# Row counts and queue order of the k, v, q and weight transfers in a fused attention and feed-forward kernel

## The chip, the cores and the metric

The kernel runs on one core of one Trainium2 chip. The metric is the device time of that core in microseconds, as the median of three runs. A profile is one further execution, recorded instruction by instruction and DMA packet by packet; its own span is 926.5 us.

## The reference

The program is a linear attention followed by a feed-forward block with a gated activation, in float32:

```python
kv  = einsum('bhsd,bhse->bhde', k, v)             # q, k, v: 8 x 8 x 576 x 64
out = einsum('bhsd,bhde->bhse', q, kv)
x   = out / sqrt(mean(out*out, -1) + 1e-6) * g_norm   # then (b,h,s,d) -> (b*s, h*d): 4608 x 512
h   = x @ w_in                                    # 512 x 2048
g   = h * erf(softplus(h))
y   = g @ w_out                                   # 2048 x 512
```

The weights reach the chip as 64-bit floats and are turned into float32 on the chip, which is why w_in and w_out are first read as pairs of 32-bit words (`w_raw`).

## The kernel before

**Tiles.** The batch of eight sequences gives nine token blocks T of 512 tokens (T = 0 to 7 hold the first 512 tokens of a sequence each, T = 8 holds the eight rests of 64). The 512 model columns are four chunks of 128, each a pair of heads; a "pair" is one T and one of its four head pairs, numbered i = 4 T + p. The 2048 hidden columns are 16 blocks f of 128.

**Two ways to multiply.** T = 0, the first two hidden blocks of T = 1 and the output of T = 1's first twelve use plain float32 matmuls and weights kept on the chip (`w_in_sb`, `w_out_sb`). Everything after that works on operands split into three forms, and a product of 512 x 128 x 512 is twelve matmuls: eight into `n_ps` and four into `m_ps` (`product`, L634). The three forms of each weight block are one tile of 128 rows of 6144 bytes (768 KB). They are made once during T = 1 (`w_upper` on ScalarE, `w_lower` on VectorE), stored to DRAM by `w_lower` (L672, or L668 for those kept in `w_in_sb`'s place), and read back for every token block by `load_parts` (L773).

**Periods.** From T = 2 on the work goes in 28 periods of four hidden blocks: m counts them, each T has four. In a period TensorE makes four hidden products (`hidden`, weights from `w_in_parts`) and then four result products (`result`, one for each 128 tokens j; each reads all four `w_out_parts` tiles of the batch of hidden blocks made a period before). Between these come pieces of the attention of the pair (T + 1, p) with p the period's number in its block: `visit` multiplies q by the kv matrix and forms the kv matrix of the next pair, `mean` and `norm` normalise, `turn` transposes the next pair's q on VectorE (L318). Which piece goes where is a list of places. In the first period of a block the four results of the block before are stored (`store`, L705).

**Buffers.** w_in_parts has four buffers: the tile of hidden block f is replaced once its product is done. w_out_parts has seven; a batch's four tiles come free together, at the end of the period's last product, since each of the four results reads all four tiles. k, v and q have two buffers for each pair in turn.

**Order of the transfers.** All of these are issued by SyncE's queue (SP), in the order in which the program is written; an instruction of SP that waits holds all that stand behind it. The strings in `FETCH` say after which of the eight products of a period a weight tile is asked for: "in" at places 1, 2, 4 and 6, "out" at 3, 5 and twice at 7, and four w_out tiles ahead of the first period. `load_pair` asks for k and v of the pair two ahead, and `load_q` (eight small transfers of 32 x 8 x 32 or 32 x 10 x 32 elements, 128 bytes a piece) for its q, at the attention's third group of pieces (places 3). In T = 0 and T = 1 they are asked for in the middle of a hidden block's work.

**Shapes of k and v.** For T > 0 the 576 rows of k are dealt out as five chunks (`chunks`): 115 rows hold five consecutive tokens each, and the one token left over is a row of its own, the second transfer of `load_pair` (L146). `kv_products` multiplies the rows in two halves, 0 to 63 and the rest. For T = 0 there are six chunks of 96 rows and no rest.

Of the kernel before, what the change touches and what calls it, by code (L numbers as in the profile page):

```python
# [49 lines left out]

BATCH = 4
LAG = 5


FIRST = 2
# [6 lines left out]
def kernel(  # L62
# [48 lines left out]
    exp_ln_table()  # L111


    q_sb, k_sb, v_sb = {}, {}, {}


    q_last = early.tile([P, 2, 2, D], FP32, name="q_last", bufs=1)
# [2 lines left out]

        return 6 if T == 0 else 5

    def load_pair(i, turned=True):
        T, p = divmod(i, NP)
        if T >= B:
            return
        pool = early if i in (2, 3) else kvp
        side = nc.scalar if i < 3 else nc.sync
        if T == 0:
            t = pool.tile([P, G if pool is early else S], FP32, name="q_sb", tag="q")  # L130
            t = q_sb[T, p] = t[:, 0:G].rearrange("p (j h d) -> p j h d", j=J, h=2)
            nc.sync.dma_start(
                out=t, in_=q[T, 2 * p : 2 * p + 2, 0:G, :].rearrange("h (p j) d -> p j h d", j=J)
            )
        for name, got, src in (("k", k_sb, k), ("v", v_sb, v)):
            C = chunks(T)
            rows, rest = divmod(S, C)
            assert rest < 2
            t = got[T, p] = pool.tile([rows + rest, 2, C, D], FP32, name=f"{name}_sb", tag=name)
            heads = src[T, 2 * p : 2 * p + 2]  # L140
            side.dma_start(
                out=t[:rows].rearrange("r h c d -> r h (c d)"),
                in_=heads[:, : S - rest].rearrange("h (r c) d -> r h (c d)", c=C),
            )
            if rest:
                side.dma_start(  # L146
                    out=t[rows:, :, 0], in_=heads[:, S - rest :].rearrange("h r d -> r h d")
                )
        if T > 0 and turned:
            load_q(i)  # L150

    def load_q(i):


        T, p = divmod(i, NP)
        t = q_sb[T, p] = kvp.tile([P, S], FP32, name="q_sb", tag="q")
        for n in range(P // SQ):
            h, w = divmod(n, D // SQ)
            to = t[n * SQ : n * SQ + SQ].rearrange("a (j b) -> a j b", b=SQ)
            for head, js in ((1 - h, slice(0, G // 2 // SQ)), (h, slice(G // 2 // SQ, S // SQ))):  # L160
                src = q[T, 2 * p + head, :, w * SQ : w * SQ + SQ]
                nc.sync.dma_start(
                    out=to[:, js], in_=src.rearrange("(j a) b -> a j b", a=SQ)[:, js]
                )

    def load_last(p):
        nc.sync.dma_start(
# [152 lines left out]
    def kv_products(T, p, at, crossed):  # L320


        ks, vs = (x.pop((T, p)) for x in (k_sb, v_sb))
        C = chunks(T)
        for c in range(C):
            for r in range(2):
                rows = (slice(0, D), slice(D, S // C + (c < S % C)))[r]
                for i in range(2):
                    yield partial(
                        nc.tensor.matmul,  # L330
                        at[rows_of[i], 1 - (r ^ i) if crossed else r, kv_cols],
                        lhsT=ks[rows, i, c],
                        rhs=vs[rows, i, c],
                        start=(c == 0),
                        stop=(c == C - 1),
                    )
# [29 lines left out]
    def attention(T, p, pools=None, in_parts=False):  # L366
# [31 lines left out]
        def products():  # L398

            kv_ps = st["kv"] = bank("kv_ps")  # L400
            ks, vs, qs = (x.pop((T, p)) for x in (k_sb, v_sb, q_sb))
            C = chunks(T)
            for c in range(C):
                rows = slice(0, S // C + (c < S % C))
                for i in range(2):
                    s = rows_of[i]
                    nc.tensor.matmul(
                        kv_ps[s, s],
                        lhsT=ks[rows, i, c],
                        rhs=vs[rows, i, c],  # L410
                        start=(c == 0),
                        stop=(c == C - 1),
                    )
            if p % 2 == 0:
                nc.tensor.transpose(kv_ps[:, q_tail], q_last[:, p // 2], ident)
            st["qT"] = square_tile("qT")
            for s in rows_of:
                nc.vector.tensor_copy(out=bd[s, s], in_=kv_ps[s, s])
            if p % 2 == 0:
                tails[T] = attp.tile([P, G], FP32, name="qT_last", tag="sq_lo")[:, 0:P]  # L420
                nc.vector.tensor_copy(out=tails[T], in_=kv_ps[:, q_tail])
            st["tail"] = tails[T][:, p % 2 * R : p % 2 * R + R]
            qt_ps = bank("qt_ps")
            for j in range(J):
                nc.tensor.transpose(qt_ps[:, j * P : j * P + P], qs[:, j], ident)
            nc.scalar.copy(st["qT"], qt_ps)
# [123 lines left out]
            split_lower()  # L550

        def loads():
            load_pair(T * NP + p + 2)

        if T == 0:
            return products, apply, halve, mean, norm
# [4 lines left out]
        first_ = (partial(prepare, T, p),) if (T, p) == (1, 0) else ()  # L561
        then_ = partial(turn, *then)
        if apart:
            pieces = (first_, (visit, halve, keep_tail), (loads, then_))
            return (*(partial(chain, *group) for group in pieces), mean, norm, *after)
        pieces = (first_, (visit, loads), (halve, keep_tail) if halves else (keep_tail,))
        return (*(partial(chain, *group) for group in pieces), mean, partial(chain, norm, then_), *after)
# [176 lines left out]
    for i in range(NP + 3):  # L744
        for piece, p in ((0, i), (1, i - 1), (4, i - 3), (3, i - 2)):
            if 0 <= p < NP:
                first[p][piece]()
        if i == 1:
            for _ in range(RAW - 2):
                w_next("load")  # L750
            load_pair(NP, turned=False)
            load_pair(NP + 1, turned=False)
        for what in w_rounds.get(i, ()):
            w_next(what)


    w_late.append(True)
    load_q(NP)
    first_batch, batches = FIRST * NB, NG * NB
    w_seq = {  # L760
        which: [(which, f) for _ in range(NG - FIRST) for f in range(FC)] for which in ("in", "out")
# [3 lines left out]
    def load_parts(which, n):  # L765


        pool = w_out_p if which == "out" and len(w_seq["out"]) > BATCH else w_in_p
        for _ in range(n):
            if w_seq[which]:  # L770
                key = w_seq[which].pop(0)
                t = pool.tile([P, 3, G], FP32, name=f"w_{which}_parts", tag="w")
                nc.sync.dma_start(out=t, in_=w_kept[key])  # L773
                w_now.setdefault(key, []).append(t)
# [47 lines left out]
    for n in range(FIRST * FC + 1):  # L822
# [58 lines left out]
        if T < FIRST:  # L881
            if n == whole:
                old_h = acc.tile([P, BATCH, G], FP32, name="h", tag="e")
            h = hs[n] = old_h[:, n - whole] if n >= whole else unit("h_sb")
            s = ss[n] = unit("s_sb")
            if n in plain:
                nc.scalar.copy(h, plain.pop(n))
            else:
                nc.scalar.activation(h, n_ps, AF.Copy, scale=SHIFT - 1.0)
                add(h, m_ps)  # L890
            if T == FIRST - 1:
                if f == 1:
                    x_both = wide.tile([P, KC, G], FP32R, name="x_both", tag="b")
                    for i in range(0, KC, 2):
                        both_only(x_high[:, i : i + 2], x_low[:, i : i + 2], x_both[:, i : i + 2])
                    x_forms[T] = x_high, x_low, x_both
                gates(done)
                for key in list(w_new):
                    w_lower(*key)
                for key in to_cut[f]:  # L900
                    w_upper(*key)
            nc.scalar.activation(s, h, AF.Softplus)
            if n == 0:
                w_next("split")
            if n == 1:
                load_q(NP + 1)
            for piece in steps[f][1]:
                piece()
            if f % BATCH == BATCH - 1:
                for i in range(n - BATCH + 1, n + 1):  # L910
                    nc.scalar.activation(ss[i], ss[i], AF.Erf)  # L911
                softplus_table()
            if T == FIRST - 1:
                load_parts("in", {FC - 3: 2, FC - 2: 1, FC - 1: 1}.get(f, 0))
# [9 lines left out]
        if T < FIRST:  # L924
            for piece in steps[f][2]:
                piece()
    for n in range(whole, FIRST * FC):
        gates(n)

# [3 lines left out]
    ctx.enter_context(tc.tile_pool(name="shift_r", bufs=1, side="right")).tile([P, 496], FP32, name="shift_r")  # L933
    late_r = ctx.enter_context(tc.tile_pool(name="late_r", bufs=1, side="right"))
    gate_r = ctx.enter_context(tc.tile_pool(name="gate_r", bufs=1, side="right"))
    w_out_p = ctx.enter_context(tc.tile_pool(name="w_out_p", bufs=7, side="right"))

    def part(h, half):
        return h[:, :, half * 2 * P : half * 2 * P + 2 * P]
# [30 lines left out]
                store(T, j, es[j], cols)  # L970


    FETCH = ("", "in", "in", "out", "in", "out", "in", "out out")
    load_parts("out", BATCH)
    g_next = []
    for m in range(first_batch, batches + 1):
        T, b = divmod(m, NB)
# [9 lines left out]
        def piece():  # L987
            if todo:
                todo.pop(0)()
# [13 lines left out]
                todo.pop(0)()  # L1003

        def fetch(place):
            for which in FETCH[place].split():
                load_parts(which, 1)


# [101 lines left out]
```

## Time and profile before

| | |
|---|---|
| median of three runs | 926.72 us (926.64 to 927.29) |
| profiled span | 926.5 us |
| HBM read, written | 224.40 MB, 34.60 MB |
| DMA packets, of these under 512 bytes | 143210, 78936 |
| SP's queue waiting for TensorE before a weight tile (L773, m_ps) | 190.9 us in 79 waits |
| SP's queue waiting for v before a q transfer (L162) | 38.6 us in 26 waits |

The page of a profile gives the busy time of each engine (PE is TensorE, PEld its weight loads, DVE VectorE, ACT ScalarE, SPq SyncE's queue). A line of a timeline begins with the start and the length in us; what stands in brackets at its end is the time for which the engine was idle before it, and what ended this. A line of the list of waits gives who waited for whom, the us in total, how often, and the longest.

### The profile page before, as it was taken

The numbers are of one execution on the slowest core, as the hardware profiler recorded it, in microseconds if no ns is written. First come the engines' busy times: TensorE is split into PE (matmuls) and PEld (weight loads), VectorE is DVE, ScalarE is ACT, GpSimd is POOL, SyncE is SP. The second block draws the span as 40 slices with busy tenths as digits, with TensorE's granted clock in tenths as the row PEclk, the third lists the DMA queues.
The fourth block names the chain that finished last, engine by engine and source line by source line (L and its number), as shares of the span: only waits on it lengthen the run. The fifth ranks groups of instructions, "written<-read, shape, count | busy, mean of one in ns | idle before, by whom it ended". The sixth has DMA issues, their size and how long they took to land.

```text
span 926.5 us, 13591 instructions
## 1 busy us (share of the span) xinstructions
PE 898.8 (97%) x4990; PEld 668.6 (72%) x4990; DVE 751.0 (81%) x1088; ACT 589.9 (64%) x783; POOL 2.4 (0%) x10
## 2 busy tenths in 40 slices
PE   6999999988999999999999999999999999999998
PEld 4444445655587888778878888788878888888886
DVE  2799958888588888888888888888888888886777
ACT  3868766767675666656665666666666766665552
POOL 1000000000000000000000000000000000000000
PEclk9999999999999999999999999999999999999999
DMA  9767506698688888988898788887889788778871
GB/s 250 237 190 265 167 1 249 246 378 313 239 287 312 311 312 310 347 308 308 308 337 309 296 310 310 301 306 284 292 313 404 272 286 322 291 288 314 325 271 51
DMA packets 143210, 259.91 MB, mean 281 GB/s; under 512 B 78936, under 2 KB 101800, under 8 KB 143144
## 3 DMA queue, kind: packets, MB, share of 16 engines
q1 hardware_dynamic: 141432, 256.74, 75.7%
q10 hardware_dynamic: 1648, 2.29, 0.9%
q8 instruction: 40, 0.66, 0.3%
q14 instruction: 26, 0.21, 0.1%
q0 software_dynamic: 64, 0.00, 0.0%
HBM read 224.40 MB, written 34.60 MB: 280 GB/s over the span
## 4 chain that ended last, share of the span: by engine, by line
PE 76%; DMA 11%; DVE 6%; ACT 5%; issue 1%; SPq 1%; DVEq 0%; ACTq 0%
PE n_ps L634 41%; PE m_ps L634 20%; PE o_ps L690 6%; PE h_ps L874 4%; DMA w_out_parts<-w_out 4%; DMA w_in_parts<-w_in 2%; DMA w_in<-w_new 2%; DMA v_sb<-in_v_dram 1%; PE at_ps L449 1%; PE at_ps L435 1%; DMA w_raw<-in_moe_w_out_dram 1%; ACT s_sb L911 1%; DMA q_sb<-in_q_dram 1%; DVE h L612 1%; PE at_ps L496 1%
## 5 line engine op out<-in xcount | busy, mean ns | idle before, releaser
L634 PE MATMUL n_ps<-w_out_parts,g_forms 128*128 128x512 f32 x928 | 231.2, 391 | 1.7 <-DMA w_out_parts<-w_out 1.7
L634 PE MATMUL n_ps<-x_forms,w_in_parts 128*128 128x512 f32 x896 | 225.1, 393 | 3.2 <-DMA w_in_parts<-w_in 2.1
L634 PEld LDWEIGHTS n_ps<-w_out_parts,g_forms 128*128 128x128 f32 x928 | 172.4, 188 | 38.4 <-DMA w_out_parts<-w_out 3.3
L634 PEld LDWEIGHTS n_ps<-x_forms,w_in_parts 128*128 128x128 f32 x896 | 166.1, 188 | 41.1 <-ACT h L1024 3.2
L1039 ACT ACTIVATE s<-h 128x512 f32<-128x512 f32 x112 | 71.0, 634 | 180.9 <-DVE h L612 180.9
L612 DVE TENSOR_TENSOR h<-m_ps,h 128x512 f32<-128x512 f32 x116 | 79.9, 689 | 61.5 <-ACT h L1024 39.9
L634 PE MATMUL m_ps<-w_out_parts,g_forms 128*128 128x512 f32 (+1 forms) x468 | 124.3, 388 | 0.0
L634 PE MATMUL m_ps<-x_forms,w_in_parts 128*128 128x512 f32 x448 | 119.8, 389 | 0.0
L690 PE MATMUL o_ps<-w_out_sb,h_sb 128*128 128x512 f32 x224 | 101.5, 596 | 0.2 <-DVE h_sb L820 0.2
L634 PEld LDWEIGHTS m_ps<-w_out_parts,g_forms 128*128 128x128 f32 x468 | 87.5, 188 | 18.4
L634 PEld LDWEIGHTS m_ps<-x_forms,w_in_parts 128*128 128x128 f32 x448 | 84.1, 188 | 17.6
L612 DVE TENSOR_TENSOR e<-m_ps,e 128x512 f32<-128x512 f32 (+1 forms) x117 | 80.3, 687 | 14.1 <-PE m_ps L634 2.9
L1024 ACT ACTIVATE h<-n_ps 128x512 f32<-128x512 f32 x112 | 65.6, 585 | 16.6 <-PE n_ps L634 16.6
L690 PEld LDWEIGHTS o_ps<-w_out_sb,h_sb 128*128 128x128 f32 x224 | 41.3, 189 | 45.3 <-issue 42.8
L578 DVE SCALAR_TENSOR_TENSOR g_forms<-g_forms 128x1024 fp32r<-128x1024 f32 x58 | 71.1, 1225 | 2.0
L575 DVE TENSOR_TENSOR g_forms<-h,g_forms 128x1024 fp32r<-128x1024 f32 x58 | 70.6, 1217 | 1.2 <-ACT g_forms L572 1.1
L572 ACT ACTIVATE g_forms<-h 128x1024 fp32r<-128x1024 f32 x58 | 58.7, 1051 | 14.8 <-PE m_ps L634 10.9
L1071 DVE TENSOR_TENSOR h<-h,s 128x1024 f32<-128x1024 f32 x56 | 65.9, 1218 | 0.0
L874 PE MATMUL h_ps<-xT,w_in_sb 128*128 128x512 f32 x144 | 64.6, 594 | 0.0
L607 DVE SCALAR_TENSOR_TENSOR e<-n_ps,e 128x512 f32<-128x512 f32 x88 | 60.1, 683 | 1.5 <-PE n_ps L634 1.5
L109 ACT ACT_TABLE_LOAD x44 | 56.5, 1283 | 0.8
L874 PEld LDWEIGHTS h_ps<-xT,w_in_sb 128*128 128x128 f32 x144 | 27.1, 190 | 33.4 <-issue 31.6
(119 smaller groups left out, 990.7 us busy)
## 6 DMA issues: line engine op xcount, KB each, us to landing
w_out_parts<-w_out SPq DMA_DIRECT2D x116, 768.0 KB
w_in_parts<-w_in SPq DMA_DIRECT2D x112, 768.0 KB
w_in<-w_new SPq DMA_DIRECT2D x16, 768.0 KB
w_raw<-in_moe_w_in_dram SPq DMA_DIRECT2D x16, 512.0 KB
w_raw<-in_moe_w_out_dram SPq DMA_DIRECT2D x8, 1024.0 KB
out_dram<-e SPq DMA_DIRECT2D x32, 256.0 KB
k_sb<-in_k_dram SPq DMA_DIRECT2D x28, 287.5 KB
v_sb<-in_v_dram SPq DMA_DIRECT2D x28, 287.5 KB
```

The source lines that it names most:

```text
L109: nc.scalar.preload_act_table_set("softplus")
L572: nc.scalar.activation(high, x, AF.Copy, scale=1.0 + 2.0**-13)
L575: nc.vector.tensor_tensor(out=low, in0=x, in1=high.bitcast(FP32), op=ALU.subtract)
L578: nc.vector.scalar_tensor_tensor(out=both, in0=low.bitcast(FP32), scalar=SHIFT, in1=high.bitcast(FP32), op0=ALU.mult, op1=ALU.add,)
L607: nc.vector.scalar_tensor_tensor(out=out_, in0=ps, scalar=scale, in1=out_, op0=ALU.mult, op1=ALU.add)
L612: nc.vector.tensor_tensor(out=out_, in0=ps, in1=out_, op=ALU.add)
L634: nc.tensor.matmul(ps[:, cols], lhsT=weights(form, k), rhs=moving(form, k)[:, cols], start=(form == forms[0] and k == 0), stop=(form == fo ...
L690: nc.tensor.matmul(o_ps[j], lhsT=g[:, j * P : j * P + P], rhs=w_out_sb[:, f, :], start=(f == 0), stop=last,)
L874: nc.tensor.matmul(plain[i], lhsT=w_in_sb[:, i % FC, c], rhs=xT[T][:, c, :], start=(c == 0), stop=(c == KC - 1),)
L1024: nc.scalar.activation(h[:, i], n_ps, AF.Copy, scale=SHIFT - 1.0)
L1039: nc.scalar.activation(s[:, i], h[:, i], AF.Softplus)
L1071: nc.vector.tensor_tensor(out=part(h, half), in0=part(h, half), in1=part(s, half), op=ALU.mult)
```

## The change

Three edits, all of them on the transfers alone:

1. `rows_in`: for T > 0 k and v come as 112 rows of five tokens, and 16 tokens more are a transfer of 16 rows into chunk 0, rows 112 to 127. `kv_products` takes 128 rows of chunk 0 and 112 of the others.
2. In the loop over periods, a period's transfers stand in blocks: k, v and q at the period's start, then four w_in (after the second, third and fourth hidden product and the first result), and four w_out at the end. Seven w_out, as many as there are buffers, are asked for ahead of the first period. The last two periods have a list of their own.
3. Before that, the transfers of q, and from the attention of T = 1 on those of k and v too, go into a list (`to_fetch`) from which two are issued after each raw weight load of T = 0, and four after each hidden block.

```diff
+OUT_BUFS = 7
+    def rows_in(T, c):
+        rows = S // chunks(T) // 16 * 16
+        return rows + (S - chunks(T) * rows if c == 0 else 0)
-    def load_pair(i, turned=True):
+    def load_pair(i, later=False):
...
-            rows, rest = divmod(S, C)
+            rows, rest = rows_in(T, 1), rows_in(T, 0) - rows_in(T, 1)
...
+            if later:
+                to_fetch.extend(due_)
+            else:
+                for start in due_:
+                    start()
-        if T > 0 and turned:
+        if T > 0:
             load_q(i)
+            if T > FIRST and not later:
+                fetch_some(P)
...
-                nc.sync.dma_start(
-                    out=to[:, js], in_=src.rearrange("(j a) b -> a j b", a=SQ)[:, js]
+                to_fetch.append(
+                    partial(
+                        nc.sync.dma_start,
...
+    def fetch_some(n):
+        for due_ in to_fetch[:n]:
+            due_()
+        del to_fetch[:n]
...
-            load_pair(T * NP + p + 2)
+            load_pair(T * NP + p + 2, later=not apart)
...
-            pieces = (first_, (visit, halve, keep_tail), (loads, then_))
+            pieces = ((loads,), (visit, halve, keep_tail), (then_,))
...
-            load_pair(NP, turned=False)
-            load_pair(NP + 1, turned=False)
+            load_pair(NP)
+            load_pair(NP + 1)
         for what in w_rounds.get(i, ()):
             w_next(what)
+            if what == "load":
+                fetch_some(2)
...
-    load_q(NP)
...
-        pool = w_out_p if which == "out" and len(w_seq["out"]) > BATCH else w_in_p
+        pool = w_out_p if which == "out" and len(w_seq["out"]) > 1 else w_in_p
...
-            if n == 1:
-                load_q(NP + 1)
...
         if T < FIRST:
             for piece in steps[f][2]:
                 piece()
+            fetch_some(4)
...
-    FETCH = ("", "in", "in", "out", "in", "out", "in", "out out")
-    load_parts("out", BATCH)
+    FETCH = ("", "in", "in", "in", "in", "", "", "out out out out")
+    FETCH_LAST = ("", "in", "in", "in", "in out", "", "", "")
+    fetch_some(P)
+    load_parts("out", OUT_BUFS)
...
-            for which in FETCH[place].split():
+            for which in (FETCH_LAST if m >= batches - 1 else FETCH)[place].split():
```

More of the change, by code (lines that the diff above doesn't have):

```diff
@@ L111 @@
     exp_ln_table()
-    q_sb, k_sb, v_sb = {}, {}, {}
+    q_sb, k_sb, v_sb, to_fetch = {}, {}, {}, []
     q_last = early.tile([P, 2, 2, D], FP32, name="q_last", bufs=1)
@@ L136, in load_pair @@
             C = chunks(T)
-            rows, rest = divmod(S, C)
-            assert rest < 2
+            rows, rest = rows_in(T, 1), rows_in(T, 0) - rows_in(T, 1)
             t = got[T, p] = pool.tile([rows + rest, 2, C, D], FP32, name=f"{name}_sb", tag=name)
             heads = src[T, 2 * p : 2 * p + 2]
[L141 to L144, printed above, removed]
-            if rest:
-                side.dma_start(
-                    out=t[rows:, :, 0], in_=heads[:, S - rest :].rearrange("h r d -> r h d")
-                )
-        if T > 0 and turned:
+            due_ = [
+                partial(
+                    side.dma_start,
+                    out=t[:rows].rearrange("r h c d -> r h (c d)"),
+                    in_=heads[:, : S - rest].rearrange("h (r c) d -> r h (c d)", c=C),
+                )
+            ]
+            if rest:
+                due_.append(
+                    partial(
+                        side.dma_start,
+                        out=t[rows:, :, 0],
+                        in_=heads[:, S - rest :].rearrange("h r d -> r h d"),
+                    )
+                )
+            if later:
[4 more added lines that the diff above has]
+        if T > 0:
             load_q(i)
+            if T > FIRST and not later:
+                fetch_some(P)
     def load_q(i):
@@ L161, in load_q @@
                 src = q[T, 2 * p + head, :, w * SQ : w * SQ + SQ]
-                nc.sync.dma_start(
-                    out=to[:, js], in_=src.rearrange("(j a) b -> a j b", a=SQ)[:, js]
-                )
+                to_fetch.append(
+                    partial(
+                        nc.sync.dma_start,
+                        out=to[:, js],
+                        in_=src.rearrange("(j a) b -> a j b", a=SQ)[:, js],
+                    )
+                )
+    def fetch_some(n):
+        for due_ in to_fetch[:n]:
+            due_()
+        del to_fetch[:n]
     def load_last(p):
@@ L326, in kv_products @@
             for r in range(2):
-                rows = (slice(0, D), slice(D, S // C + (c < S % C)))[r]
+                rows = (slice(0, D), slice(D, rows_in(T, c)))[r]
                 for i in range(2):
@@ L403, in products @@
             for c in range(C):
-                rows = slice(0, S // C + (c < S % C))
+                rows = slice(0, S // C)
                 for i in range(2):
@@ L935 @@
     gate_r = ctx.enter_context(tc.tile_pool(name="gate_r", bufs=1, side="right"))
-    w_out_p = ctx.enter_context(tc.tile_pool(name="w_out_p", bufs=7, side="right"))
+    w_out_p = ctx.enter_context(tc.tile_pool(name="w_out_p", bufs=OUT_BUFS, side="right"))
     def part(h, half):
```

## The prediction, made before the changed kernel was run

> **What bounds the kernel now.** I read the page's head first, then the waits of TensorE, then what the DMA engines did in single stretches, last the DMA queue of SyncE (SP).
>
> ```profile
> span 926.5 us, 13591 instructions
> ...
> PE 898.8 (97%) x4990; PEld 668.6 (72%) x4990; DVE 751.0 (81%) x1088; ACT 589.9 (64%) x783; POOL 2.4 (0%) x10
> ```
>
> TensorE is busy for 97% of the span. What a new order of transfers can give back lies in the other 27.7 us. The waits of TensorE's matmuls (us in total, times, longest) say which part a transfer ended; w_in_parts and w_out_parts are read from 254 us on, in the loop over whole token blocks:
>
> ```profile
> PE n_ps L634 <- DMA w_in_parts<-w_in: 2.1, 2, 1.7
> PE at_ps L435 <- DVE qT L318: 2.0, 1, 2.0
> PE n_ps L634 <- DMA w_out_parts<-w_out: 1.7, 2, 0.9
> ...
> PE n_ps L634 <- ACT h L1024: 0.8, 1, 0.8
> ```
>
> The rest is mostly the start, where T=0's k and v come on ACT's queue, and two gaps of 3.4 and 2.8 us behind ACT. The timeline of TensorE puts the four weight waits at 386, 483, 599 and 672 us:
>
> ```profile
> 387.14 0.72 PE L634 MATMUL n_ps<-w_out_parts,g_forms 128*128 128x512 f32 x2 [0.76 <-DMA w_out_parts<-w_out]
> ...
> 484.05 0.73 PE L634 MATMUL n_ps<-w_out_parts,g_forms 128*128 128x512 f32 x2 [0.91 <-DMA w_out_parts<-w_out]
> ...
> 601.13 1.17 PE L634 MATMUL n_ps<-x_forms,w_in_parts 128*128 128x512 f32 x4 [1.70 <-DMA w_in_parts<-w_in]
> ...
> 673.28 0.93 PE L634 MATMUL n_ps<-x_forms,w_in_parts 128*128 128x512 f32 x3 [0.44 <-DMA w_in_parts<-w_in]
> ```
>
> They sit about a token block (four periods) apart, near the block's stores: a sign of a DMA side that is just full when stores come on top. Busy time by stretch shows why (the last two columns are the DMA engines' mean share and GB/s):
>
> ```profile
> 22.00:27.00 5.00, 3.94 (x10) 1.33 (x9) 4.50 (x9) 4.94 (x10) 0.00 (x0) 1.00 0.35 127
> 46.00:51.00 5.00, 3.01 (x57) 1.69 (x56) 3.21 (x4) 4.94 (x8) 0.00 (x0) 1.00 0.39 65
> 256.00:267.00 11.00, 11.00 (x95) 8.64 (x94) 7.98 (x14) 5.53 (x11) 0.00 (x0) 1.00 1.00 410
> ```
>
> From 22 to 27 us only k and v of 115 rows are under way: 0.35 of 16 engines, that is five or six, and 127 GB/s. From 256 to 267 us only weight tiles are: all 16, 410 GB/s. From 46 to 51 us it is q in pieces of 128 bytes. SP's queue in one period:
>
> ```profile
> 288.68 3.09 SPq L146 DMA_DIRECT2D v_sb<-in_v_dram  x1
> 291.82 8.57 SPq L162 DMA_DIRECT2D q_sb<-in_q_dram  x8
> 300.43 0.46 SPq L773 DMA_DIRECT2D w_out_parts<-w_out  x1
> ```
>
> Eight small q transfers hold the queue for 8.57 us, and every weight tile behind them waits.
>
> [...] No run shows 112 yet, but the 128-row tiles fill all 16. [...] The built program gives SP's transfers eight semaphores in turn, so each waits for the eighth before it; the queue's waits agree (q waits for v 38.6 us in all, for w_in_parts 23.1, for k 16.7).
>
> **The change part by part.** The order of instructions on TensorE, VectorE, ScalarE and GpSimd is the same in both programs; only SP's transfers differ in shape and order. I sum against the profiled span of 926.5 us; the timed runs have a median of 926.72, so I add 0.2.
>
> *1. 112 + 16 rows.* One of k or v is 115 x 2 x 320 x 4 = 294 KB: at 127 GB/s 2.3 us, 4.6 us for both. On 16 engines I take the tiles' 410 GB/s: 0.7 us each, 1.5 us for both with the 16-row rests (bounds 1.4 and, if 1280-byte pieces or the rests cost double, 3). A weight tile of 786 KB takes 786/410 = 1.92 us. A pair's q is 295 KB; 46 to 51 us moved 325 KB in 5 x 0.39 = 1.95 us of all engines, so 1.8 us. A period is 8 tiles, k, v and q: on the five engines 15.4 + 4.6 + 1.8 = 21.8 us before, 18.7 us after. TensorE needs 8 products of 2.72 us (268 to 276 us: three in 8.18 us) and some 2 us of attention, 23.8 us. A block's four stores (1.05 MB, 2.6 us) make it 24.4 before: over 23.8, hence the waits at block ends. After it is 21.3. So the four waits should go: 0.76 + 0.91 + 1.70 + 0.44 = 3.8 us, and since records of 0.39 us start every 0.227 us each gap hides another 0.16 us: 4.4 us. Bounds: 0 (if other waits take their place) and 4.4.
>
> *2. The order in blocks.* Time 0 is a period's end, when the last product frees four w_out tiles. Before, w_in and w_out came mixed, around k, v, q. Now SP issues four w_out (0.45 us each), k, v, q, then four w_in. The first w_out issued is the fourth tile of the next batch; it lands at about 1.3 (from 254.26 us to the engines being full, by the packets) + 1.9 + 0.5 to 1.3 (landing after the last packet, by the semaphores at 258 to 269 us) = 4.5 and is read at about 14: four products (10.9), 2 of attention, six matmuls (1.4). w_out is safe. q waits by its semaphores for w_out, k and v to land: w_out done by 9.0, k and v by 10.5, landed by 11.5, the last q issued by 13.3, first w_in issued by 13.7, landed by 13.7 + 1.3 + 1.9 + 1.0 = 18. Needed at 23.8: 6 us to spare; with stores, 2.6 + up to 1 us more, still 2. The next three follow every 1.9 us against 2.7 us of a product. Cost nothing; the products of the running period hide it. k, v and q themselves are for two pairs later: hidden.
>
> *3. The first period.* Here seven w_out are asked for at 254.26 us, not four, and the next w_in stand behind them. Before, two w_in stood right behind four w_out and nothing waited at 275.9 us. Now: engines full from 255.6, seven tiles to 269.1, landed by 270.5; k and v to 270.6, landed by 272; then q4 to q7, first w_in issued at 273.7, landed at 273.7 + 1.0 + 1.9 + 1.0 = 277.6. TensorE wants it at 275.9 (start of the batch's second period): a new wait of 1.7 us. From below 0.5 (if landing takes 0.5 and q is quick), from above 3. In its favour: at 286.3 us the kernel before waits 0.75 us for ACT, which gains that time; with the hidden 0.16 that is 0.9 back. Net loss 0.8.
>
> *4. q of pair (1,0) earlier.* It is issued between the raw weights, not behind the second 1 MB of w_out, and k and v ahead no longer hold five engines from 22 to 33 us. Before:
>
> ```profile
> 47.72 0.78 DVE L318 STREAM_TRANSPOSE qT<-q_sb 128x576 f32<-128x576 f32 x1 [3.91 <-DMA q_sb<-in_q_dram]
> ...
> 48.65 0.66 PE L435 MATMUL at_ps<-qT,bd_kv 64*64 64x256 f32 x8 [1.99 <-DVE qT L318]
> ```
>
> SP issued the second w_out at 36.09. Now all but two of the q stand ahead of it, and these two land by about 42 (36.5 + rest of the w_in 1.5 + 2.5 for 1 MB at 410 GB/s + 1.5). VectorE is free at 43.8, so the transpose ends at 44.6, before TensorE's earlier matmuls end at 46.66. Gain 1.9. ACT's next pieces (table load at 47.09, w_m at 48.39) do not depend on q and leave VectorE the w_out block by about 51, where the o_ps matmuls would now start (51.6). Bounds 0.5 and 2.0.
>
> *5. q in fours between the stores of the new weights.* At 177 to 184.7 us eight q stand ahead of two stores, and ACT then waits for buffers:
>
> ```profile
> 177.41 7.30 SPq L162 DMA_DIRECT2D q_sb<-in_q_dram  x8
> 184.82 0.39 SPq L672 DMA_DIRECT2D w_out<-w_new  x1
> ```
>
> ```profile
> 188.13 0.63 ACT L596 ACTIVATE w_new<-w_out_sb 128x512 fp32r<-128x512 f32 x1 [1.44 <-DMA w_out<-w_new]
> 190.12 0.63 ACT L596 ACTIVATE w_new<-w_in_sb 128x512 fp32r<-128x512 f32 x1 [1.36 <-DMA w_in<-w_new]
> ```
>
> The chain behind it (softplus, table, erf, table, next evacuation) ends in TensorE's gap of 3.4 us at 194. The stores go first now; but the second buffer is also read by a product until about 189.5, so only 0.6 us comes back, and nothing at 224 us, where a product holds the buffer until 220.0. Bounds 0 and 1.
>
> Sum: -4.4 + 0.8 - 1.9 - 0.6 = -6.1 us. 926.7 - 6.1 = **920.6 us**.
>
> **The rivals.**
> - *Absorbed* (13%): without the pauses VectorE (86% busy in these stages, the 285.6 us wait) and ACT fall behind, and TensorE waits for them as long as it did for transfers. Then part 1 gives nothing, parts 4 and 5 stay and part 3 costs nothing: 926.7 - 2.5 = 924.2. Against it: periods without a transfer wait take 23.8 us and have no ACT wait, so VectorE keeps up there.
> - *Late w_in* (9%, the other side): w_in stands last, behind q. If the eight q still take the 8.57 us of before once w_out has landed at 10.5, the first w_in is issued at 19.4 and lands at 23.3, 12.8 us after w_out. An ordinary period allows 23.8 - 10.5 = 13.3 us; one with stores 2.6 less, 10.7. So each of the four later periods with stores is 2.1 us late, 8.4 in all: 929.0. That is where it decides: under 10.7 us nothing is lost, from 12.8 us on it is slower, at 14 us sixteen ordinary periods lose 0.7 and four 3.3, 24 us. For it: q has always been slow on the queue. Against: what q waited for were k and v at 2.3 us each on five engines, and this falls to a third.
> - *Not spread* (4%): the 112 rows still run on few engines. Then k and v cost 3.1 us more in a chain with 6 (with stores 2) to spare: four periods 1.1 us late, part 1's 4.4 not gained, part 3 worse by 1.5: 920.6 + 4.4 + 4.4 + 1.5 = 930.9.
> - *Everything goes* (12%): no wait in part 3, the ACT waits too: 926.7 - 4.4 - 0.9 - 2.0 - 1.0 = 918.4.
>
> **How the numbers follow.** The forecast has 62%, its own range 919.0 to 923.0 (part 3 at 3, part 4 at 0.5: 923.3; part 3 at 0.5: 919.4). Runs of this kernel differ by 0.65 us; 0.2%, or 1.9 us, is about what can be told from no change: faster is below 924.9, slower above 928.6. Faster: 62 + 12 + 10 of *absorbed* = 84%. Same: 3 of *absorbed*, 4 of *late w_in* = 7%. Slower: 5 of *late w_in*, 4 of *not spread* = 9%. The range 918.0 to 925.0 holds the forecast, *everything goes* and nearly all of *absorbed*; it leaves out some 17%.
>
> **What would show it.** In the changed profile: k and v alone at a DMA share near 1, not 0.35 (part 1); no w_parts waits at block ends after 380 us; a w_in wait near 274 us of 0.5 to 3 us (part 3); no wait for qT near 47 us; SP's eight q in under 5 us and waiting for w_out. I am wrong if w_in waits come every period, if new ACT waits equal to the old DMA waits appear, or if the stage before 254 us, where k and q move past the stores, gets longer.

## The result, and the profile after

Before, 927.00 us (median of 4 runs, 926.64 to 929.40); after, **922.75 us** (median of 4, 921.88 to 923.70). The ratio is 0.9949, 95% interval 0.9929 to 0.9968. The profiled execution after has a span of 921.0 us against 926.5. (The one before took 928.31 us when timed, 1.3 us above its median, so the spans lie 5.5 us apart and the medians 4.25.) So the change is faster by about half a per cent, as forecast; how the sum came about is another matter. Below, *before* and *after* are also the names of the two kernels and their profiles.

The head of the page after, and the row of the clock that TensorE was granted in each fortieth of the span (23 us):

```profile
span 921.0 us, 13656 instructions
...
PE 899.1 (98%) x4990; PEld 670.1 (73%) x4990; DVE 750.3 (81%) x1088; ACT 589.8 (64%) x783; POOL 2.4 (0%) x10
...
PEclk9999999999989999999999999999999999999999
```

TensorE's idle time fell from 27.7 us to 21.9. The 8 in the twelfth slice of the clock (253 to 276 us) is new; before has nines throughout. The waits of TensorE's matmuls after the change:

```profile
PE n_ps L662 <- DMA w_in_parts<-w_in: 3.7, 1, 3.7
...
PE at_ps L524 <- DVE bd_kv L369: 1.4, 3, 0.6
...
PE at_ps L524 <- DVE x_last L485: 1.0, 1, 1.0
```

The four weight waits at 386, 483, 599 and 672 us, the wait for w_out and the wait for q's transpose are gone. What stands instead is one wait for w_in, in the loop's second period, and four waits for VectorE that the kernel before did not have. (The matmul that waits there is the mean's; bd_kv and x_last name the VectorE instruction that was the last to end before it.) TensorE's and SP's timelines around the first:

```profile
266.85 1.07 PE L662 MATMUL m_ps<-w_out_parts,g_forms 128*128 128x512 f32 x4
271.63 3.75 PE L662 MATMUL n_ps<-x_forms,w_in_parts 128*128 128x512 f32 x8 [3.71 <-DMA w_in_parts<-w_in]
275.18 1.91 PE L662 MATMUL m_ps<-x_forms,w_in_parts 128*128 128x512 f32 x4
276.88 2.22 PE L662 MATMUL n_ps<-x_forms,w_in_parts 128*128 128x512 f32 x8
```

```profile
257.57 8.99 SPq L191 DMA_DIRECT2D q_sb<-in_q_dram  x8
266.66 2.13 SPq L802 DMA_DIRECT2D w_in_parts<-w_in  x4
268.89 1.62 SPq L733 DMA_DIRECT2D out_dram<-e  x3
```

The first product after the wait takes 3.75 us for eight matmuls that take about 2 us elsewhere: it runs at half clock. Two stretches of 2 us show the same in the ninth value, the granted clock (0.63 and 0.50); the others are those of the start that the prediction showed of before (the DMA share and GB/s are the last two):

```profile
22.00:27.00 5.00, 3.73 (x10) 1.74 (x11) 4.64 (x9) 4.87 (x10) 0.00 (x0) 1.00 0.83 222
46.00:51.00 5.00, 5.00 (x58) 2.69 (x53) 4.43 (x9) 4.96 (x7) 0.00 (x0) 1.00 0.87 270
...
270.00:272.00 2.00, 0.37 (x1) 0.40 (x2) 1.97 (x4) 0.15 (x1) 0.00 (x0) 0.63 0.97 402
272.00:274.00 2.00, 2.00 (x6) 1.52 (x6) 1.97 (x2) 0.00 (x0) 0.00 (x0) 0.50 1.02 422
```

From 22 to 27 us, where k and v of 115 rows kept 0.35 of the engines busy, 112 rows and what follows them keep 0.83 busy and move 222 GB/s instead of 127; TensorE no longer waits from 46 to 51 us. After the change k and v are done by 26 us, and raw weights and q come in. In the one microsecond from 23 us on only packets of k and v run in both kernels, first before, then after:

```profile
23.00:24.00 1.00, 0.86 (x2) 0.49 (x3) 0.84 (x3) 1.00 (x3) 0.00 (x0) 1.00 0.33 122
```

```profile
23.00:24.00 1.00, 1.00 (x5) 0.59 (x4) 0.97 (x3) 0.97 (x3) 0.00 (x0) 1.00 1.08 295
```

All 16 engines are busy then, at 295 GB/s.

TensorE runs the same 4990 matmuls in the same order in both programs, so each can be compared with itself. By how much it comes earlier after the change ("the lead") is a ledger of the whole difference. In us, times on the clock of after:

| stretch | what happens | change of the lead | forecast |
|---|---|---|---|
| to 40 us | start of the program; 1.11 of it by 17 us, when the first transfers of another shape have just been issued | +1.12 | 0 |
| 45 to 55 us | the wait for q of pair (1,0) goes (part 4) | +1.73 | +1.9 |
| 192 and 219 us | two gaps behind ScalarE shrink, 3.4 to 0.9 and 2.8 to 0 (part 5) | +5.24 | +0.6 |
| 268 to 272 us | w_in is late (part 3) | -3.87 | -1.7 |
| 272 to 277 us | half clock | -2.73 | 0 |
| 284 us | a wait for ScalarE goes (part 3) | +1.01 | +0.9 |
| 383, 479, 595, 667 us | the four weight waits (part 1) | +4.92 | +4.4 |
| other places, nearly all after 285 us | small differences, most of them waits that go | +1.36 | 0 |
| 430, 526, 622, 718 us | waits for VectorE come | -3.28 | 0 |
| sum | | +5.50 | +6.1 |

The first row is scatter of the start: in the other kernels of this study, whose start is the same, the lead at 40 us lay between -0.8 and +1.1. The largest gain stands at two gaps of TensorE, which the kernel before has at 194 and 224 us, and of which one is left after:

```profile
197.25 0.49 PE L634 MATMUL n_ps<-x_high,w_new 128*128 128x512 f32 x1 [3.42 <-ACT h_sb L889]
...
227.12 0.50 PE L634 MATMUL n_ps<-x_high,w_new 128*128 128x512 f32 x1 [2.79 <-ACT h L889]
```

```profile
191.93 0.50 PE L662 MATMUL n_ps<-x_high,w_new 128*128 128x512 f32 x1 [0.86 <-ACT h_sb L918]
```

### The profile page after: what moved, and what is told of

The parts are those of the page before. It is cut to its first block, busy times and chain, and to the rows that moved or that the text cites. A ratio compares the mean times of both kernels' runs of the same rounds, so it can differ in the third digit from the quotient of the medians.

```text
span 921.0 us, 13656 instructions
## 1 busy us (share of the span) xinstructions
PE 899.1 (98%) x4990; PEld 670.1 (73%) x4990; DVE 750.3 (81%) x1088; ACT 589.8 (64%) x783; POOL 2.4 (0%) x10
## 4 chain that ended last, share of the span: by engine, by line
PE 74%; DVE 11%; DMA 6%; ACT 5%; issue 3%; SPq 1%; DVEq 0%
PE n_ps L662 39%; PE m_ps L662 19%; PE h_ps L903 6%; PE o_ps L718 5%; DMA v_sb<-in_v_dram 3%; PE at_ps L477 1%; DVE e L640 1%; PE at_ps L463 1%; DVE h L640 1%; DMA q_sb<-in_q_dram 1%; DVE g_forms L603 1%; DVE w_new L627 1%; ACT s_sb L938 1%; DVE h L1101 1%; DVE h_sb L640 1%
## 6 DMA issues: line engine op xcount, KB each, us to landing
out_dram<-e SPq DMA_DIRECT2D x32, 256.0 KB, 6.1
k_sb<-in_k_dram SPq DMA_DIRECT2D x28, 280.0 KB, 10.2
```

## The experiments

In all of them the kernel before was run beside on the same chip, and ratios are to it; its medians there are 929.6 us, so ratios compare better than times. In each of these 37 executions of it the mean granted clock was 0.994 to 0.998, while the profiled one had 1.000: the kernel before usually loses some clock as well. `rows_only` had 0.999 or 1.000 in all of its runs. So part of what the row counts give there may be clock that is no longer lost, which the profiled pair cannot show; no trace of such an execution was kept.

**The two parts of the change, each alone.** `rows_only` is before with the row counts of the change and nothing else of it:

```diff
+    def rows_in(T, c):
+        rows = S // chunks(T) // 16 * 16
+        return rows + (S - chunks(T) * rows if c == 0 else 0)
...
-            rows, rest = divmod(S, C)
+            rows, rest = rows_in(T, 1), rows_in(T, 0) - rows_in(T, 1)
...
-                rows = (slice(0, D), slice(D, S // C + (c < S % C)))[r]
+                rows = (slice(0, D), slice(D, rows_in(T, c)))[r]
```

> The kernel before with k and v as 112 + 16 rows, its queue order unchanged. Theory (the row counts free five engines, which were full at block ends): the four weight waits in the loop (4.4 us) go, of which up to 2.4 us come back as waits for VectorE as in the changed kernel; q lands earlier at 47 us (2 us); no wait of 4 us at the second period, since two w_in still stand right behind four w_out. About 921 to 923 us. Rival (the queue order is what helps): the four waits stay within 1 us of what they were and the time is 926 us or more.

`order_only` is after with 115 + 1 rows again:

```diff
-        rows = S // chunks(T) // 16 * 16
+        rows = S // chunks(T)
```

> The changed kernel with k and v as 115 + 1 rows again; the queue order in blocks stays. Theory: k and v take 3.1 us more of the five engines in front of the four w_in, so w_in comes late in periods with stores and the wait at the second period grows from 3.9 to some 7 us; the four old waits do not all go: about 926 to 932 us. Rival (order alone does it): no wait for w_in but the one at the second period, 923 to 924 us. The gaps at 194 and 224 us (3.4 and 2.8 us before, 0.9 and 0 after) tell which part removed them: gone here means the order of q and the stores, still here means the row counts.

Measured: `rows_only` 918.01 us (917.74 to 919.32), ratio 0.9884 (0.9857 to 0.9910), the profiled span 916.3; `order_only` 934.69 us (930.01 to 937.53), ratio 1.0057 (1.0036 to 1.0077), span 934.0. The head of `rows_only`, and its waits for VectorE; then the first wait of `order_only`:

```profile
span 916.3 us, 13591 instructions
...
PE at_ps L500 <- DVE bd_kv L345: 1.2, 2, 0.6
PE at_ps L500 <- DVE x_last L461: 0.9, 1, 0.9
```

```profile
PE n_ps L662 <- DMA w_in_parts<-w_in: 11.4, 6, 5.4
```

The stretch from 22 to 27 us, of `rows_only` and then of `order_only`:

```profile
22.00:27.00 5.00, 3.75 (x10) 1.58 (x10) 4.64 (x9) 4.91 (x10) 0.00 (x0) 1.00 1.08 281
```

```profile
22.00:27.00 5.00, 3.68 (x10) 1.58 (x10) 4.64 (x9) 4.91 (x10) 0.00 (x0) 1.00 0.46 158
```

The row counts alone make the kernel faster than the whole change does. The rest of the change, the blocks and the seven tiles asked for ahead of them, is a loss on top: with 115 rows w_in is late six times, 11.4 us, and with 112 rows once. What row counts decide shows in the DMA share of the same five microseconds: 0.83 and 1.08 with 112, 0.35 and 0.46 with 115. The two gaps at 194 and 224 us shrink in both kernels (to 0.93 and 0.52 in `rows_only`, to 0.93 and 1.16 in `order_only`), so either part is enough for what the prediction called part 5.

**Is the surplus of three w_out tiles the cause of the late w_in?** Seven w_out instead of four are asked for ahead of the loop. `first_four` asks for four, and for the other three behind the first period's w_in:

```diff
-    load_parts("out", OUT_BUFS)
+    load_parts("out", BATCH)
...
+            if m == first_batch and place == BATCH:
+                load_parts("out", OUT_BUFS - BATCH)
```

> The changed kernel, but four w_out tiles ahead of the first period and the other three behind its four w_in. Theory: the 3.9 us wait for w_in at 268 us is three tiles of 1.92 us too many in front, and the slow matmuls after it (clock 0.75 from 267 to 274 us, 2.7 us lost) come from that idle time; both go, less 0.9 us that ACT's chain takes back: about 917 us. Rival (absorbed): VectorE or ACT fill the gap, less than 2 us gained: 921 us or more. If the clock dips without the wait, the second half of the theory falls.

Measured: 923.21 us (922.45 to 925.63), ratio 0.9928 (0.9910 to 0.9947). No wait at 268 us; instead one of 1.03 us for w_out at 259 us and, one period on:

```profile
296.27 3.75 PE L662 MATMUL n_ps<-x_forms,w_in_parts 128*128 128x512 f32 x8 [3.10 <-DMA w_in_parts<-w_in]
```

The wait has moved, half clock and all (3.75 us for the eight matmuls again). `ramp` spreads the three tiles over three periods, one each:

```diff
-    load_parts("out", OUT_BUFS)
+    load_parts("out", BATCH)
...
+            if m < first_batch + OUT_BUFS - BATCH and place == BATCH:
+                load_parts("out", 1)
```

> The changed kernel with four w_out ahead of the first period, and one more than four in each of the first three periods. Theory: three more tiles are 5.8 us of the DMA engines, which one period cannot give and three can (each has 5 us free, the first, with its stores, 2.5): the wait at the second period is 0 to 1 us, no half clock, span 916 to 918.5 us. Rival (the block order is late in every early period whatever is ahead): a wait of 2 us or more between 265 and 320 us, span 920 us or more.

Measured: 919.38 us (918.93 to 919.80), ratio 0.9876 (0.9841 to 0.9911), span 917.8. Its waits for weights:

```profile
PE n_ps L662 <- DMA w_out_parts<-w_out: 1.4, 1, 1.4
...
PE n_ps L662 <- DMA w_in_parts<-w_in: 0.9, 2, 0.7
```

No wait is longer than 1.4 us, the mean granted clock of the profiled execution is 1.0, and the span is within 1.5 us of `rows_only`; by their ratios (0.9876 and 0.9884) the two are not told apart, so without the surplus the blocks show neither gain nor loss. So, within the order in blocks, the surplus is the cause: seven w_out, k, v, q and four w_in are more than one period's transfers leave room for. Seven tiles ahead of the old mixed order were not run. `w_in_first` leaves the seven ahead and moves the first period's k, v and q behind its w_in:

```diff
-            load_pair(T * NP + p + 2, later=not apart)
+            if (T, p) != (FIRST + 1, 0):
+                load_pair(T * NP + p + 2, later=not apart)
...
+            if m == first_batch and place == BATCH:
+                load_pair((FIRST + 1) * NP + 2)
```

> The changed kernel, but in the first period alone k, v and q stand behind the four w_in. Theory: what the blocks cost against the row counts alone (spans of 921.0 and 916.3 us) is one event, the late w_in of the second period with the half clock after it. k, v and q and the waits of q for the semaphores of w_out take some 5 to 7 us out of w_in's way, so it lands near 264 to 265 us, before 268: no wait, no half clock, span 916 to 917.5 us. Rival (too much is asked for at once, as when four w_out went ahead and the wait moved to 293 us): the wait shows up a period later and the span stays at 920 us or more.

Measured: 924.23 us (923.27 to 925.86), ratio 0.9936 (0.9911 to 0.9960). The wait at 268 us is gone, and w_in is late at 294.8 us by 3.77 us, again with a loss of clock (mean granted clock 0.995, as in after). SP's queue says why: the q passed over here are issued until 275 us, and the next period's stand in front of its w_in:

```profile
265.99 9.06 SPq L191 DMA_DIRECT2D q_sb<-in_q_dram  x8
...
284.52 8.98 SPq L191 DMA_DIRECT2D q_sb<-in_q_dram  x8
293.60 2.10 SPq L803 DMA_DIRECT2D w_in_parts<-w_in  x4
```

Another order within one period is thus not the remedy: in `first_four` and here the wait has only moved.

**The half clock.** `warm` gives TensorE 15 more matmuls to do while w_in is awaited:

```diff
+        if idle and idle.pop():
+            for _ in range(15):
+                nc.tensor.matmul(
+                    n_ps, lhsT=moving(0, 0)[:, 0:P], rhs=moving(0, 0), start=True, stop=True
+                )
```

> The changed kernel with 15 matmuls more (3.4 us, results overwritten) ahead of the second period's first hidden product, where TensorE waits 3.9 us for w_in. Theory (the half clock follows from the idle time): TensorE waits under 1 us at one piece, the clock stays at 1.0, and the 2.7 us of slow matmuls are gained: span 918.3 us. Rival (the clock falls for another reason, or the matmuls come on top): the clock still dips or the span is 921 us or more.

Measured: 923.42 us (922.80 to 927.37), ratio 0.9928 (0.9896 to 0.9961), span 921.4. The row of the clock, and the wait a period later:

```profile
PEclk9999999999999999999999999999999999999999
```

```profile
298.71 1.63 PE L667 MATMUL n_ps<-x_forms,w_in_parts 128*128 128x512 f32 x6 [1.86 <-DMA w_in_parts<-w_in]
```

The half clock is gone (mean granted clock 0.999 against 0.995 in after), so it came from the idle TensorE. But the 2.73 us did not come back: counted from 227 us on, `warm` is 2.7 us better off than after at 280 us, 0.6 at 305 us, and 0.9 at the end, where after has lost 2.5 us of lead and `warm` 1.6 (one profiled execution each; the times of the two do not differ beyond their intervals). While TensorE ran at half speed the transfers had caught up; at full speed it waits 1.86 us for w_in a period later.

**The waits for VectorE.** They come at the block-end mean, whose operands VectorE prepares. Is it the place of the mean, or VectorE's load? `mean_later` puts the mean of a block's last period one place further on:

```diff
-            places = (0, 0 if T + 1 == B else 2, 2 if T + 1 == B else 3, 4, 5, 5, 6)
+            places = (0, 0 if T + 1 == B else 2, 2 if T + 1 == B else 3, 5, 5, 5, 6)
```

> The changed kernel with the mean of a block's last period one product later. Theory: the four new waits for VectorE (430, 526, 622, 717 us, 2.4 us in all) are waits of this mean for pieces that VectorE reaches late; with 2.7 us more they go and 1 to 2.4 us are gained: 920.4 to 921.8 us. Rival: VectorE is short of time over the whole period, so the wait moves to the next block's first product: same time as the changed kernel, 922.8, or slower.

Measured: 936.91 us (936.18 to 938.00), ratio 1.0085 (1.0058 to 1.0113). A miss for the theory that a later place would do:

```profile
PE n_ps L662 <- DVE e L635: 8.8, 6, 2.0
```

TensorE now waits for VectorE elsewhere, and longer, as the rival had it. `after_less_vector` and `less_vector` take work from VectorE, one instruction of 692 ns a period, the first from after and the second from `rows_only`:

```diff
-            add(es[j][:, cols], ps[1][:, cols])
+            if j != 2 or T == NG - 1:
+                add(es[j][:, cols], ps[1][:, cols])
```

> The changed kernel, with one VectorE instruction of 692 ns left out in each period but the last ones: the third result's sum no longer takes in its second half (m_ps), so these outputs lack that part. It stands late in a period, and the mean that waits at a block's end comes in the next period behind it. Theory (TensorE's waits of 0.33 to 1.0 us for VectorE at 430, 526, 622 and 717 us are VectorE being short over the periods, so 0.7 us less work a period pays them back): all four go, 2.4 us, and nothing takes their place; a span near 918.5 against 921.0 us, ratio near 0.992. The wait for w_in at 268 us (3.7 us) and the slow clock after it stay. Rival (the four waits come from where the mean stands in the block's order, behind the evacuation of kv and x_last, and are set by TensorE's and ScalarE's own pace, not by VectorE's load): at least three of the four stay above 0.2 us, and the span stays within 0.7 us of 921.0.

> The kernel with the row counts alone, with the same VectorE instruction left out in each period (692 ns; the third result lacks its second half). With the row counts alone TensorE waits for VectorE at 520.9 (0.57), 616.9 (0.59) and 712.3 us (0.95), 2.1 us, and the span is 916.3 us. Theory (VectorE's load): all three go, a span near 914.2 us, ratio near 0.9865. Rival (the order, not the load): at least two stay, a span within 0.7 us of 916.3. Third possibility: the waits go and a wait for a weight tile takes their place, since TensorE now asks for weights 2 us earlier than before; then a w_in or w_out wait of 0.5 us or more shows after 500 us.

Measured: `after_less_vector` 920.17 us (918.39 to 920.66), ratio 0.9903 (0.9871 to 0.9935), span 916.4; `less_vector` 915.52 us (914.98 to 916.86), ratio 0.9854 (0.9826 to 0.9881), span 914.9. The head of each, and the longest wait that is left in the loop:

```profile
PE 897.0 (98%) x4990; PEld 669.9 (73%) x4990; DVE 735.1 (80%) x1063; ACT 589.3 (64%) x783; POOL 2.4 (0%) x10
...
PE n_ps L662 <- DMA w_in_parts<-w_in: 3.5, 1, 3.5
```

```profile
PE 895.9 (98%) x4990; PEld 668.8 (73%) x4990; DVE 734.7 (80%) x1063; ACT 589.1 (64%) x783; POOL 2.4 (0%) x10
...
PE n_ps L638 <- DMA w_in_parts<-w_in: 0.8, 1, 0.8
```

Neither has a wait for bd_kv or x_last. By their times alone the two pairs are not told apart, since the intervals overlap; the traces, one of each kernel, do it. Matmul by matmul, the lead over the same kernel with all of VectorE's work grows at the four means by 0.45, 0.78, 0.79 and 1.15 us in after (3.2 in all) and by 0.48, 0.76, 0.78 and 1.12 in `rows_only` (3.1). It is VectorE's load: with less of it the waits go, with the mean in its old place. The third possibility, that weight waits take their place, did not come about: the wait for w_in of 0.8 us stands at 281 us. (The first span fell by 4.6 us, as in that execution the half clock lasted 3.41 us and not 6.83, which gave 1.3 more. The second fell by only 1.4 us, since that execution lost 1.8 us at the start and at q's transpose near 47 us.)

**Rows and the early order together, without blocks.** `mixed_loop` is after with the loop's transfers as before:

```diff
-    FETCH = ("", "in", "in", "in", "in", "", "", "out out out out")
+    FETCH = ("", "in", "in", "out", "in", "out", "in", "out out")
...
-    load_parts("out", OUT_BUFS)
+    load_parts("out", BATCH)
...
-            pieces = ((loads,), (visit, halve, keep_tail), (then_,))
+            pieces = (first_, (visit, halve, keep_tail), (loads, then_))
```

> Row counts as 112 + 16 and the changed order of q, k and v before the loop, but the loop's transfers in the old, mixed order. Theory: the stage before the loop gains 0.8 us over the row counts alone (lead at 227 us 8.0 against 7.2 us), the loop is the same: span 915.5 us, the fastest so far. Rival: the early order only moves waits that ACT and VectorE then fill: 916.3 us as with the row counts alone, or slower.

Measured: 918.52 us (917.91 to 918.63), ratio 0.9865 (0.9823 to 0.9907), span 916.8, one wait for w_in of 0.81 us. It equals `rows_only` within the intervals: from 40 to 227 us `rows_only` gains 6.4 us, `mixed_loop` 6.8, after 6.9 and `order_only` 5.0. The early order adds nothing to the row counts that these runs can show.

The best versions that compute the whole reference are `rows_only`, `mixed_loop` and `ramp`, at 918.0 to 919.4 us; they are not told apart, and the interval of each lies below that of after.

## Why the prediction was right, and where its sum was wrong

The time, the sign and the range held. Two terms were wrong by almost 5 us each, in opposite directions: part 5 gave 4.6 us more than forecast, part 3 cost 4.8 more. That the total was right is the luck of their cancelling. The step from a span to a time was wrong as well: the prediction adds 0.2 us, but the profiled execution before was timed at 928.31 us for a span of 926.5, and that after at 922.80 for 921.0, 1.8 us more each. In spans the forecast is 920.4 against 921.0; in times it is a gain of 6.1 us against 4.25.

1. *Rows.* Right in kind and size. The 112 rows use the engines that the 115 leave idle: the share from 23 to 24 us, with k and v alone, went from 0.33 to 1.08, at 295 GB/s where the prediction took 410. Of other row counts, and of what sets the number of engines, these runs show nothing. The four waits gave 4.9 us, forecast 4.4. But the rival *absorbed* (13%) was true for two thirds of it: 3.3 us came back as waits for VectorE. The argument against it, that VectorE keeps up in periods without a transfer wait, looked at single periods; over a block, with the mean at its end, VectorE has no such room, as the two kernels with less work for it show. Small waits that the prediction did not count gave 1.4 us, so part 1 gave 3.0 net.
2. *Blocks.* No cost in an ordinary period, as forecast, and for the reason given: w_out asked for at 345.35 us, the first w_in at 360.14, 14.8 us later (forecast 13.7, *late w_in* 19.4), and the first product that reads it at 369.64. Wrong was "SP's eight q in under 5 us": in the loop they take 7.7 to 10.2 us, waiting for w_out to land:

```profile
345.35 2.31 SPq L802 DMA_DIRECT2D w_out_parts<-w_out  x4
347.71 1.01 SPq L165 DMA_DIRECT2D k_sb<-in_k_dram  x2
348.77 1.01 SPq L165 DMA_DIRECT2D v_sb<-in_v_dram  x2
349.94 10.10 SPq L191 DMA_DIRECT2D q_sb<-in_q_dram  x8
360.14 1.99 SPq L802 DMA_DIRECT2D w_in_parts<-w_in  x4
```

   The blocks bring no gain either: `rows_only` has the old order and none of the four waits. SP's waits for TensorE before a weight tile did not shrink, 223.8 us against 190.9, and q's waits are now for w_out:

```profile
SPq L802 <- PE m_ps L662: 223.8, 92, 11.8
SPq L191 <- DMA w_out_parts<-w_out: 119.7, 65, 3.8
```

3. *The first period.* The failed term. A wait was forecast at the right product and for the right reason, at 1.7 us with 3 as its upper bound; it was 3.7. On the clock of after, 8.0 us ahead, the forecast was: w_in issued at 265.7, landed at 269.6. It was issued at 266.66, 1.0 late, behind q's 8.99 us, and landed at about 271.5, 4.8 us after its issue and not 3.9. The sum of single steps (0.5 to 1.3 us of landing, 1.9 of transfer) took the tile as if it had the engines to itself; over all w_in tiles after the change the median from issue to landing is 7.4 us. What the sum lacked altogether is the half clock that came with the wait, 2.73 us: the prediction had a wait bounded at 3 us without asking about the clock. In the profile after, the granted clock fell to 0.5 at 270.5 us, 2.6 us into the wait, and stayed there for 6.83 us. Net, part 3 cost 5.6 us and not 0.8.
4. *q of (1,0).* Right: 2.1 us at the wait, of which 0.3 is lost again at 55 us; forecast 1.9.
5. *q between the stores.* Undersized: 5.2 us against 0.6, bounds 0 and 1. The wait for the stores' buffers was seen, but what holds ScalarE was summed as if the product that reads the second buffer stood fixed. Before, ScalarE waits for stores by 1.44, 1.36, 0.35, 1.54 and 2.15 us from 188 to 218 us, and at 220.00 for that product by 1.31; after, only one such wait is left, 0.34 us at 195.56. That the product came earlier because the gap at 194 was gone fits this, and no run shows it by itself. On SP two stores go ahead of the q after the change, as forecast:

```profile
175.35 0.34 SPq L700 DMA_DIRECT2D w_out<-w_new  x1
176.68 0.34 SPq L700 DMA_DIRECT2D w_in<-w_new  x1
177.11 3.24 SPq L696 DMA_DIRECT2D w_out<-w_in_sb  x3
180.40 2.28 SPq L191 DMA_DIRECT2D q_sb<-in_q_dram  x4
182.79 0.39 SPq L700 DMA_DIRECT2D w_out<-w_new  x1
183.29 0.36 SPq L700 DMA_DIRECT2D w_in<-w_new  x1
```

   The store that stood at 184.82 us, behind eight q, is issued at 175.35 (the one at 182.79 is the next, at 189.26 before). Less the lead of 2.8 us that there was already, it comes 6.7 us earlier. But it isn't this order that is needed: in `rows_only` all eight q still go first, and the same store is issued at 179.51, since the q hold the queue for 4.32 us and not 7.30; in `order_only` it is issued at 176.40. Each of the two edits suffices, and the prediction gave the gain to the order alone.

Of the rivals, *late w_in* as it was drawn, in every block with stores, came true only with 115 rows (`order_only`: six waits for w_in, of them one in each of three blocks from 499 us on, of 0.65 to 1.86 us); *not spread* is excluded by the DMA share (1.08 from 23 to 24 us); *everything goes* did not come about, since the wait for w_in came.

Left open: what of the 3.3 us at VectorE is the mean's own chain and what the whole block's load; and the start's scatter, up to 1.9 us between kernels, which no run here explains.

## What to carry to other kernels

Cost the shape of a transfer and the order of transfers as two changes, and try each alone: here the first brought all of the gain and the second took back some 4.7 us of profiled span, by the seven tiles asked for at once. A stretch in which a queue is asked for more than its period carries (here seven tiles where buffers come free, though only four are needed soon) had to be spread over several periods; moving it within one only moved the wait. When several waits are to go, look for the engine that is next, over the whole block, before counting them as gained; and price a long wait of TensorE with the slower clock that may come with it: here one of 3.71 us came with 6.83 us at half clock.

## What was not expected of the hardware

*When the clock halves.* The profile after has full speed for 256.0 us, half for 6.83, then full for 641.71; the clock fell within the wait of 3.71 us for w_in. In `first_four` the wait of 3.10 us for w_in came with a clock of 0.50 from 296 to 302 us, and in `after_less_vector` one of 3.53 us with 3.41 us of half clock. In `order_only` the product behind a wait of 5.39 us took 3.75 us for its eight matmuls, as in after. But the gap of 3.42 us at 194 us in the kernel before cost no clock: it was 1.00 from 190 to 198 us. So a wait's length alone does not tell its price: 3.10 us cost clock and 3.42 us did not. On what else it depends these runs do not show. The timed runs of after differ too: their mean clock was 0.995 in two and 0.998 in two, as in the traces with 6.83 and with 3.41 us of half clock.

*A slow engine can help the one that feeds it.* The half clock's 2.73 us were for the larger part time that the transfers needed anyway: with the clock kept at full speed, `warm` gained 0.9 us of it at the most.
